# Depthwise convolution in 32x32 tiles of the PE array, with rows of h turned by DMA and PSUM in eight one-bank slots

## The chip, the cores and the metric

The kernel runs on one core of a Trainium2 chip. The metric is the device time of one execution in microseconds. Three runs of the kernel before gave 276.89, 278.99 and 280.02 us; their median is 278.99 us.

The engines are named as in the profile: PE (TensorE matmuls), PEld (its weight loads), DVE (VectorE), ACT (ScalarE), POOL (GpSimd) and SP (SyncE, which issues nearly all DMAs).

## The reference

Sliding-window attention (window 32 to both sides) over 8 batches, 8 heads, 576 positions and head dimension 64, and then a feed-forward block with a depthwise convolution of three taps along the sequence:

```python
scores = scale * np.matmul(q, k.transpose(0, 1, 3, 2))
mask = np.abs(pos[:, None] - pos[None, :]) <= 32
attn = softmax(np.where(mask, scores, -1e9))
x = np.matmul(attn, v)                       # to (8, 576, 512)

h = np.maximum(x @ w_in, 0.0)                # (8, 576, 1024)
conv_out = sum(conv_w[k] * shifted(h, k - 1) for k in range(3))   # per channel
gate = 1.0 / (1.0 + np.exp(-conv_out))
out = (h * gate) @ w_out                     # (8, 576, 512)
```

Inputs and the output are float32; the kernel multiplies in bf16.

## The kernel before

**Attention.** The heads of a batch are worked in four pairs `g`. `load_qk` and `load_v` bring float32 into staging tiles, POOL casts them to bf16 (`cast`). `job_tr` transposes the q or k of two pairs by nine matmuls against the identity each into one three-bank PSUM slot, and ACT and DVE copy one half each. (For batch 0 it does so in three pieces of 4, 4 and 1 blocks.) `job_sc` makes the scores of a pair, 18 matmuls of 64 rows, two heads one above the other in the array; ACT takes the exponential (1088 columns and 64), DVE multiplies by the band mask. `job_av` multiplies with v, 20 matmuls of 64 output columns; DVE normalises into `xn`. From batch 1 on, v shifted by 64 rows (`vo`) is made by two DMAs inside SBUF (`shift_v`). `job_xt` transposes `xn` into `xT`.

**Feed-forward.** The sequence of two batches is cut into three chunks `c` of 384 rows; there are twelve chunks. A chunk has eight blocks `m` of 128 channels. `job_ph` makes a block of h: four matmuls against `w_in`, and ACT's relu, halved, into `hT`. `job_pc` convolves the block: three matmuls, one for each tap, against a 128x128 diagonal matrix `diag_w` (built on DVE by `make_diag`, 24 in all), accumulated in PSUM; ACT takes the tanh into `tn`, and DVE forms the gated block `gT` = (`tn` + 1) * `hT`. Chunk 1 is worked in two halves of 192 columns. `job_py` makes 128 output rows: eight matmuls of `gT` against `w_out`, a copy by ACT into `y_sb`, and an output DMA.

**PSUM.** `psum_a` is one slot of three banks (transposes and scores), `psum_f` five slots of one bank (all else).

**Order.** The function `at` gives each job a planned time and the jobs that must come before it, and `give_out` emits the jobs by planned time. `P` = 29 is the planned time of a batch, `PC` = 2P/3 that of a chunk, and `dm` = `PC`/9 = 2.15. In the plan of a chunk, `ph` of block m stands at m `dm`, and the three outputs of the chunk before at 2.7, 5.3 and 7.9 `dm`. DMAs and POOL's casts keep this order. So do the compute engines for jobs planned before `T0` + 14 = 37 (`InOrder`, which is why early instructions carry line 87); later ones are ordered by the scheduler. Every engine executes its own list strictly in order, and so does SP: a DMA that waits holds up those behind it.

Of the kernel before, what the change touches and what calls it, by code (L numbers as in the profile page):

```python
# [17 lines left out]
def kernel(  # L18
# [51 lines left out]
    diag_w = consts.tile([128, 3, MB, 128], BF16, name="diag_w")  # L70
# [73 lines left out]
    conv_w24 = consts.tile([3 * MB, 128], FP32, name="conv_w24")  # L144
    nc.scalar.dma_start(conv_w24, moe_conv_w.rearrange("k (m p) -> (k m) p", p=128))
    make_identity(nc, ident)
    ident24 = consts.tile([3 * MB, 3 * MB], FP32, name="ident24")
    nc.vector.tensor_copy(out=ident24, in_=ident[0:3 * MB, 0:3 * MB])
    nc.vector.memset(mask1, 1.0)
# [30 lines left out]
    def load_weight(src, dst, rows, cast_):  # L180

        n = src.shape[1] // 2
        for x in (0, n):
            st = {}

            def load(x=x, st=st):
                t_ = fpool.tile([128, rows * n], FP32, name="wst", tag="wst")
                st[0] = t_.rearrange("p (c f) -> p c f", c=rows)
                fixed(nc.sync.dma_start(
                    st[0], src.rearrange("(c p) f -> p c f", p=128)[:, :, x:x + n]  # L190
                ))
# [9 lines left out]
    def slot_a():  # L201
        return psum_a.tile([128, 1536], FP32, name="pa", tag="pa")

    def slot_f():
        return psum_f.tile([128, 512], FP32, name="pf", tag="pf")
# [4 lines left out]
    def job_tr(g2, y):  # L210

        b, i = g2 // NPH, g2 % NPH
        nat = qkb_pp[b % NLD][y][i]
        to = []
        for g in (2 * g2, 2 * g2 + 1):
            if y == 0:
                t_ = apool.tile([128, S], BF16, name="qT", tag="qT", bufs=4)
                to.append(t_)
            else:
                t_ = kT_pp[g % NKT]  # L220
                to.append(t_[:, PAD:PAD + S])
            state["qk"[y], g] = t_

        small = b == 0
        for js in ((range(0, 4), range(4, 8), range(8, RP)) if small else (range(RP),)):
            j0, n = js[0], len(js)
            ps = slot_f() if small else slot_a()
            for j in js:
                tensor.matmul(  # L229
                    ps[:, 128 * (j - j0):128 * (j - j0) + 128],  # L230
                    nat[:, j, :, :].rearrange("p e d -> p (e d)"),
                    ident, start=True, stop=True,
                )
            rows = ps[:, 0:128 * n].rearrange("p (j y x) -> p y x j", j=n, y=2)
            for x, copy in enumerate((scalar.copy, vector.tensor_copy)):
                copy(  # L236
                    out=to[x].rearrange("p (x j) -> p x j", j=RP)[:, :, j0:j0 + n], in_=rows[:, x]
                )
# [9 lines left out]
    def col(e, t):  # L248

        return 512 * e + 64 * t if t < 8 else 1024 + 64 * e  # L250

    def job_sc(g):
        qT, kT = state.pop(("q", g)), state.pop(("k", g))
        ps, last = slot_a(), slot_f()
        for i in range(NT):
            for e, t in ((0, (i + NT - 1) % NT), (1, i)):
                tensor.matmul(  # L257
                    last[:, 0:64] if e * t == NT - 1 else ps[:, col(e, t):col(e, t) + 64],
                    kT[64 * e:64 * e + 64, 64 * t:64 * t + 128],
                    qT[64 * e:64 * e + 64, 64 * t:64 * t + 64],  # L260
                    start=True, stop=True,
                )
        attn = apool.tile([128, 2 * S], BF16, name="attn", tag="attn", bufs=4)
        state["a", g] = attn
        x = 2 * S - 64
# [99 lines left out]
    def job_pc(c, m, halves=(0, 1)):  # L365
        kind = c % 3
        step = HW + (2 if kind == 1 else 0)
        if m == 0 and halves[0] == 0:
            gT[c] = fpool.tile([128, MB, CH], BF16, name="gT", tag="gT", bufs=3)

        def taps(kk):
            base = hT_pp[kind][:, m, kk:kk + HW]
            return bass.AP(
                base.tensor, base.offset + step * halves[0],
                [list(base.ap[0]), [step, len(halves)], [1, HW]],
            )

        n = HW * len(halves)
        ps = slot_f()
        for kk in range(3):  # L380
            tensor.matmul(  # L381
                ps[:, 0:n], diag_w[:, kk, m, :], taps(kk), start=(kk == 0), stop=(kk == 2)
            )
        tn = spool.tile([128, CH], FP32, name="tn", tag="tn")
        scalar.activation(tn[:, 0:n], ps[:, 0:n], AF.Tanh, bias=0.0, scale=1.0)  # L385
        vector.scalar_tensor_tensor(  # L386
            out=gT[c][:, m, HW * halves[0]:HW * halves[0] + n].rearrange(
                "p (i x) -> p i x", x=HW),
            in0=tn[:, 0:n].rearrange("p (i x) -> p i x", x=HW), scalar=1.0, in1=taps(1),
            op0=ALU.add, op1=ALU.mult,  # L390
        )

    out_rows = out.rearrange("b s f -> (b s) f")

# [23 lines left out]
    def at(key, t, job, *before):  # L418
        assert key not in plan
        plan[key] = (t, job, before)  # L420
# [29 lines left out]
    def hidden(c, t, dt, part):  # L450
        halves = (0, 1) if part is None else (part,)
        kind = c % 3
        b0 = c // 3 * 2
        need = []
        if kind < 2 and part != 1:
            need += [("xt", b0, i) for i in (range(4) if kind == 0 else range(NBLK))]
        if kind and part != 0:
            need += [("xt", b0 + 1, i) for i in (range(2) if kind == 1 else range(NBLK))]
        for m in range(MB):
            at(("ph", c, m, part), t + m * dt, lambda m=m: job_ph(c, m, halves),  # L460
               *need, ("w_in", 2 * m // MB),
               *[("pc", c - 3, m, x) for x in (None, 0, 1)])
            at(("pc", c, m, part), t + (m + 1.4) * dt, lambda m=m: job_pc(c, m, halves),
               ("ph", c, m, part), ("diag", m), *[("py", c - 3, i) for i in range(3)],
               *[("pc", c, m, x) for x in (0,) if part == 1])

    for m in range(MB):
        at(("diag", m), (8.8, 9.0, 11.7)[m] if m < 3 else T0 + 1.6 * m - 1.5, lambda m=m: make_diag(m), ("conv_w",))
    at(("conv_w",), 7.0, job_conv_w)
    for c in range(NCH):  # L470
        if c == 0:
            hidden(0, T0, 1.6, None)
        elif c == 1:
            hidden(1, T0 + 13.0, 1.0, 0)
            hidden(1, start[1], 1.4, 1)
        else:
            hidden(c, start[c], dm, None)
        for i in range(3):
            t = start[c + 1] + (2.7 + 2.6 * i) * dm if c else T1 + 2.0 + 3.0 * i
            at(("py", c, i), t, lambda c=c, i=i: job_py(c, i),  # L480
               *[("pc", c, m, x) for m in range(MB) for x in (None, 0, 1)], ("w_out", 0), ("w_out", 1))


    pair = {}
# [58 lines left out]
    for i, (ld, cs) in enumerate(load_weight(moe_w_out, w_out_sb, MB, cast)):  # L543
# [33 lines left out]
```

## Time and profile before

| what | value |
|---|---|
| times of three runs | 276.89, 278.99, 280.02 us |
| median | 278.99 us |
| profiled execution | span 274.9 us from the first to the last instruction |
| PE busy | 243.0 us, 88% |
| DVE busy | 179.0 us, 65% |
| ACT busy | 174.4 us, 63% |
| POOL busy | 81.2 us, 30% |
| SP's DMA queue | 45.68 MB, 59.4% of the 16 DMA engines |
| mean granted PE clock | 0.988 |

The profile gives the execution's span alone; what lies around the span is seen from the median, which is 4.1 us longer. Times inside the profile count from the start of the span. A busy share is a mean over the whole span; the prediction reads the stages apart from each other, because the first 66 us, the steady part and the end have different limits.

### The profile page before, as it was taken

The page shows a single profiled execution, that of the slowest core. Times are in us where ns is not written, and L with a number is a line of the kernel's source. Part 1 is how long each engine was busy: PE and PEld are TensorE (multiplying, and loading weights), DVE is VectorE, ACT ScalarE, POOL GpSimd, SP SyncE. Part 2 cuts the span into 40 slices and gives each one's busy share as a digit, 9 for nine tenths or more (in the row PEclk, how much of TensorE's full clock was granted, in tenths as well). Part 3 has the DMA queues.
Part 4 walks back from the last instruction along what each step waited for, and adds up shares of the span by engine and source line. Part 5 has one row for each costly group of instructions (what it writes and reads, how often), then busy time and mean ns, then how long its engine had stood idle before and what let it go on. Part 6 is the DMA issues. An engine that isn't in the chain of part 4 may idle for free.

```text
span 274.9 us, 6658 instructions
## 1 busy us (share of the span) xinstructions
PE 243.0 (88%) x2654; PEld 149.9 (55%) x2682; DVE 179.0 (65%) x392; ACT 174.4 (63%) x370; POOL 81.2 (30%) x96
## 2 busy tenths in 40 slices
PE   0746975886999999999999999999999999999994
PEld 0625444564665665656566555565566655555551
DVE  5697385996567688687667858696576656623230
ACT  1756472575678667767777677576776766556552
POOL 5659666664125143134113503333200000000000
PEclk9999996899999999999999999999999999999999
DMA  6999999996486925956659556974241211112123
GB/s 244 242 294 387 211 305 326 222 316 151 124 200 244 247 62 114 251 192 171 155 154 310 150 123 162 270 195 118 67 118 38 74 43 41 42 38 76 41 76 114
DMA packets 55714, 46.11 MB, mean 168 GB/s; under 512 B 38892, under 2 KB 40964, under 8 KB 55684
## 3 DMA queue, kind: packets, MB, share of 16 engines
q1 hardware_dynamic: 55648, 45.68, 59.4%
q8 instruction: 21, 0.34, 0.5%
q14 instruction: 9, 0.07, 0.1%
q10 hardware_dynamic: 36, 0.01, 0.0%
HBM read 32.52 MB, written 9.44 MB: 153 GB/s over the span
## 4 chain that ended last, share of the span: by engine, by line
PE 69%; DMA 11%; DVE 8%; SPq 4%; ACT 3%; issue 3%; POOL 1%
PE pf L399 22%; PE pf L343 19%; PE pf L381 14%; DMA kst<-in_k_dram 5%; PE pa L229 4%; PE pf L282 4%; DMA vst<-in_v_dram 4%; SPq L95 3%; DMA vo<-ve 3%; PE pa L257 3%; PE pf L313 2%; DVE xT L318 2%; DVE attn L268 2%; DVE gT L386 1%; DVE gT L87 1%
## 5 line engine op out<-in xcount | busy, mean ns | idle before, releaser
L386 DVE SCALAR_TENSOR_TENSOR gT<-tn,hT 128x384 bf16<-128x384 f32 (+1 forms) x96 | 56.8, 599 | 45.9 <-ACT tn L385 45.5
L343 PE MATMUL pf<-xT,w_in_sb 128*128 128x385 bf16 (+2 forms) x380 | 73.4, 315 | 2.3 <-DVE xn L301 1.4
L399 PE MATMUL pf<-w_out_sb,gT 128*128 128x512 bf16 x260 | 65.6, 379 | 1.4
L381 PE MATMUL pf<-hT,diag_w 128*128 128x384 bf16 (+1 forms) x288 | 58.7, 313 | 0.7 <-ACT hT L354 0.6
L404 ACT COPY y_sb<-pf 128x512 f32<-128x512 f32 x36 | 21.1, 586 | 42.5 <-PE pf L399 40.2
L385 ACT ACTIVATE tn<-pf 128x384 f32<-128x384 f32 (+1 forms) x96 | 45.1, 470 | 4.2 <-PE pf L381 3.4
L343 PEld LDWEIGHTS <-w_in_sb 128*128 128x128 bf16 x380 | 33.9, 98 | 21.9 <-DVE xn L301 2.0
L399 PEld LDWEIGHTS <-gT 128*128 128x128 bf16 x288 | 27.8, 98 | 29.6 <-DVE gT L386 0.2
L109 POOL TENSOR_SCALAR ve<-vst 128x512 bf16<-128x512 f32 x40 | 29.3, 736 | 49.3 <-DMA vst<-in_v_dram 40.2
L381 PEld LDWEIGHTS <-diag_w 128*128 128x128 bf16 x288 | 25.8, 97 | 15.7 <-issue 1.1
L363 ACT ACTIVATE hT<-pf 128x385 bf16<-128x385 f32 x56 | 27.8, 497 | 8.7 <-PE pf L343 7.9
L266 ACT ACTIVATE attn<-pa 128x1088 bf16<-128x1088 f32 x26 | 28.0, 1076 | 5.6 <-PE pf L257 4.8
L109 POOL TENSOR_SCALAR kb<-kst 128x1152 bf16<-128x1152 f32 x16 | 20.2, 1262 | 29.3 <-DMA kst<-in_k_dram 16.3
L109 POOL TENSOR_SCALAR qb<-qst 128x1152 bf16<-128x1152 f32 x16 | 18.9, 1179 | 29.9 <-DMA qst<-in_q_dram 29.1
L268 DVE TENSOR_TENSOR attn<-attn,mask 128x1152 bf16<-128x1152 bf16 x26 | 22.3, 857 | 7.2 <-ACT attn L267 6.6
L301 DVE TENSOR_TENSOR xn<-pf,rec 128x320 bf16<-128x320 f32 x52 | 23.4, 480 | 0.4
L318 DVE CAST xT<-pf 128x512 bf16<-128x512 f32 (+1 forms) x32 | 19.2, 633 | 3.6 <-PE pf L313 3.5
L358 ACT ACTIVATE hT<-pf 128x386 bf16<-128x386 f32 x24 | 11.8, 499 | 5.4 <-PE pf L343 5.2
L282 PEld LDWEIGHTS <-attn 128*64 128x64 bf16 x520 | 10.6, 111 | 8.3 <-issue 6.0
L282 PE MATMUL pf<-ve,attn 128*64 128x65 bf16 x312 | 13.8, 197 | 0.5 <-DVE attn L268 0.3
L292 DVE RECIPROCAL rec<-pf 128x5 f32<-128x5 f32 x52 | 8.6, 181 | 7.8 <-PE pf L282 7.8
L257 PE MATMUL pa<-qT,kT 64*128 64x64 bf16 x442 | 12.5, 191 | 0.9 <-DVE kT L236 0.9
(84 smaller groups left out, 271.0 us busy)
## 6 DMA issues: line engine op xcount, KB each, us to landing
qst<-in_q_dram SPq DMA_DIRECT2D x16, 576.0 KB, 7.0
kst<-in_k_dram SPq DMA_DIRECT2D x16, 576.0 KB, 7.2
out_dram<-y_sb SPq DMA_DIRECT2D x36, 256.0 KB, 2.2
vst<-in_v_dram SPq DMA_DIRECT2D x24, 256.0 KB, 4.1
vo<-ve SPq DMA_DIRECT2D x14, 260.0 KB, 6.3
vst<-in_v_dram SPq DMA_DIRECT2D x16, 192.0 KB, 4.9
wst<-in_moe_w_in_dram SPq DMA_DIRECT2D x2, 1024.0 KB, 8.0
wst<-in_moe_w_out_dram SPq DMA_DIRECT2D x2, 1024.0 KB, 8.2
```

What stands on the lines that cost most here:

```text
L109: fixed(nc.gpsimd.tensor_scalar(out=out_, in0=in_, scalar1=1.0, scalar2=0.0, op0=ALU.mult, op1=ALU.add))
L266: scalar.activation(attn[:, 0:x], ps[:, 0:x], AF.Exp, bias=0.0, scale=scale)
L268: vector.tensor_tensor(out=attn, in0=attn, in1=mask, op=ALU.mult)
L282: tensor.matmul(pss[e][64 * j:64 * j + 64, 65 * c:65 * c + 65], attn[:, col(e, t):col(e, t) + 64], (ve if t % 2 == 0 else vo)[:, t // 2, h ...
L301: vector.tensor_tensor(out=to, in0=po[:, :, 0:64], in1=rec[:, :, None].broadcast_to([128, NBLK, 64]), op=ALU.mult,)
L318: (vector.tensor_copy if b > 1 or c % 2 else scalar.copy)(out=xT[b // 2][:, :, b % 2, 128 * c:128 * c + cols], in_=ps[:, :, 0:cols])
L343: tensor.matmul(ps[:, 0:n], w_in_sb[:, kc, m * 128:(m + 1) * 128], x_[:, kc, x0:x1], start=(kc == 0), stop=(kc == KC - 1),)
L363: scalar.activation(hT[:, m, o0:o0 + n], ps[:, 0:n], AF.Relu, bias=0.0, scale=0.5)
L381: tensor.matmul(ps[:, 0:n], diag_w[:, kk, m, :], taps(kk), start=(kk == 0), stop=(kk == 2))
L385: scalar.activation(tn[:, 0:n], ps[:, 0:n], AF.Tanh, bias=0.0, scale=1.0)
L386: vector.scalar_tensor_tensor(out=gT[c][:, m, HW * halves[0]:HW * halves[0] + n].rearrange("p (i x) -> p i x", x=HW), in0=tn[:, 0:n].rearr ...
L399: tensor.matmul(ps, gT[c][:, m, 128 * i:128 * i + 128], w_out_sb[:, m, :], start=(m == 0), stop=(m == MB - 1),)
```

## The change

- The convolution works four channel blocks at once (a quad `qd`). Each 128x128 diagonal matrix holds only four 32x32 diagonals that matter, so each tap of a block becomes four matmuls of 32 rows by 32 columns. Row group r of block m goes to column group (r + m) mod 4: the sixteen matmuls of a tap use sixteen different 32x32 tiles of the array, and the four row groups that share a column group write to four different PSUM banks.
- The channels of block m so come out turned by 32 (m mod 4) partitions. For three of the four blocks, `hT` is therefore copied into `gT` by two DMAs each, turned in the same way (`turn`), and DVE gates in place. The rows of `w_out` are turned when they are loaded: seven DMAs for each half instead of one.
- The quad needs four PSUM slots at once. `psum_a` goes, and `psum_f` has eight slots of one bank. Scores take four slots and four exponentials (512, 512, 64, 64 columns), and every `job_tr` works in three pieces as batch 0's did.
- `diag_w` is 32 wide and built by a single DVE instruction. `tn` has six buffers instead of three.
- In the plan, `pc` of quad `qd` stands at (4 `qd` + 4.4) `dm`.

```diff
-    psum_a = ctx.enter_context(tc.tile_pool(name="psum_a", bufs=1, space=bass.MemoryType.PSUM))
-    psum_f = ctx.enter_context(tc.tile_pool(name="psum_f", bufs=5, space=bass.MemoryType.PSUM))
+    psum_f = ctx.enter_context(tc.tile_pool(name="psum_f", bufs=8, space=bass.MemoryType.PSUM))
...
-    def make_diag(m):
-        for kk in range(3):
-            vector.tensor_scalar(
-                out=diag_w[:, kk, m, :], in0=ident,
-                scalar1=conv_w_sb[:, kk, m:m + 1], scalar2=None, op0=ALU.mult,
-            )
+    def make_diag():
+        vector.tensor_tensor(
+            out=diag_w.rearrange("p k m x -> p (k m) x"),
+            in0=ident32[:, None, :].broadcast_to([128, 3 * MB, 32]),
+            in1=conv_w_sb.rearrange("p k m -> p (k m)")[:, :, None].broadcast_to([128, 3 * MB, 32]),
+            op=ALU.mult,
+        )
...
+                rows_ = src.rearrange("(c p) f -> p c f", p=128)[:, :, x:x + n]
+                for s in range(4):
+                    for lo, to, cnt in turn(s):
+                        fixed(nc.sync.dma_start(
+                            st[0][to:to + cnt, s:rows:4, :], rows_[lo:lo + cnt, s:rows:4, :]
+                        ))
...
+    def turn(s):
+        return [(0, 32 * s, 128 - 32 * s), (128 - 32 * s, 0, 32 * s)][:2 if s else 1]
...
-        for js in ((range(0, 4), range(4, 8), range(8, RP)) if small else (range(RP),)):
+        for js in (range(0, 4), range(4, 8), range(8, RP)):
...
-        scalar.activation(attn[:, 0:x], ps[:, 0:x], AF.Exp, bias=0.0, scale=scale)
-        scalar.activation(attn[:, x:], last[:, 0:64], AF.Exp, bias=0.0, scale=scale)
+        for i, (x, n) in enumerate(((0, 512), (512, 512), (1024, 64), (1088, 64))):
+            scalar.activation(
+                attn[:, x:x + n], ps[i][:, 0:n], AF.Exp, bias=0.0, scale=scale
+            )
...
-        ps = slot_f()
+        ms = range(4 * qd, 4 * qd + 4)
+        for m in ms:
+            for lo, to, cnt in turn(m % 4) if m % 4 else []:
+                fixed(nc.sync.dma_start(gate(m, to, to + cnt), taps(m, 1, lo, lo + cnt)))
+        pss = [slot_f() for _ in ms]
         for kk in range(3):
-            tensor.matmul(
-                ps[:, 0:n], diag_w[:, kk, m, :], taps(kk), start=(kk == 0), stop=(kk == 2)
-            )
-        tn = spool.tile([128, CH], FP32, name="tn", tag="tn")
-        scalar.activation(tn[:, 0:n], ps[:, 0:n], AF.Tanh, bias=0.0, scale=1.0)
...
+            for ps, m in zip(pss, ms):
+                for r in range(4):
+                    o = 32 * ((r + m) % 4)
+                    tensor.matmul(
+                        ps[o:o + 32, 0:n], diag_w[32 * r:32 * r + 32, kk, m, :],
+                        taps(m, kk, 32 * r, 32 * r + 32), start=(kk == 0), stop=(kk == 2),
+                    )
+        for ps, m in zip(pss, ms):
+            tn = spool.tile([128, CH], FP32, name="tn", tag="tn", bufs=6)
+            scalar.activation(tn[:, 0:n], ps[:, 0:n], AF.Tanh, bias=0.0, scale=1.0)
+            vector.scalar_tensor_tensor(
+                out=gate(m), in0=tn[:, 0:n].rearrange("p (i x) -> p i x", x=HW), scalar=1.0,
+                in1=gate(m) if m % 4 else taps(m, 1), op0=ALU.add, op1=ALU.mult,
             )
...
+        for qd in range(MB // 4):
+            at(("pc", c, qd, part), t + (4 * qd + 4.4) * dt, lambda qd=qd: job_pc(c, qd, halves),
+               *[("ph", c, 4 * qd + m, part) for m in range(4)], ("diag",),
+               *[("py", c - 3, i) for i in range(3)],
+               *[("pc", c, qd, x) for x in (0,) if part == 1])
```

More of the change, by code (lines that the diff above doesn't have):

```diff
@@ L69 @@
     conv_w_sb = consts.tile([128, 3, MB], FP32, name="conv_w_sb")
-    diag_w = consts.tile([128, 3, MB, 128], BF16, name="diag_w")
+    diag_w = consts.tile([128, 3, MB, 32], BF16, name="diag_w")
+    ident32 = consts.tile([128, 32], BF16, name="ident32")
     ident = consts.tile([128, 128], BF16, name="ident")
@@ L146 @@
     make_identity(nc, ident)
+    for r in range(4):
+        nc.vector.tensor_copy(
+            out=ident32[32 * r:32 * r + 32, :], in_=ident[32 * r:32 * r + 32, 32 * r:32 * r + 32]
+        )
     ident24 = consts.tile([3 * MB, 3 * MB], FP32, name="ident24")
@@ L188, in load @@
                 st[0] = t_.rearrange("p (c f) -> p c f", c=rows)
-                fixed(nc.sync.dma_start(
-                    st[0], src.rearrange("(c p) f -> p c f", p=128)[:, :, x:x + n]
-                ))
+                rows_ = src.rearrange("(c p) f -> p c f", p=128)[:, :, x:x + n]
+                if not turned:
+                    fixed(nc.sync.dma_start(st[0], rows_))
+                    return
+                for s in range(4):
[3 more added lines that the diff above has]
+                        ))
             def casts(x=x, st=st):
@@ L250, in col, with bank @@
         return 512 * e + 64 * t if t < 8 else 1024 + 64 * e
+    def bank(e, t):
+        return (e, 64 * t) if t < 8 else (2 + e, 0)
     def job_sc(g):
         qT, kT = state.pop(("q", g)), state.pop(("k", g))
-        ps, last = slot_a(), slot_f()
+        ps = [slot_f() for _ in range(4)]
         for i in range(NT):
             for e, t in ((0, (i + NT - 1) % NT), (1, i)):
+                at_, x = bank(e, t)
                 tensor.matmul(
-                    last[:, 0:64] if e * t == NT - 1 else ps[:, col(e, t):col(e, t) + 64],
+                    ps[at_][:, x:x + 64],
                     kT[64 * e:64 * e + 64, 64 * t:64 * t + 128],
@@ L378, in job_pc, with gate @@
         n = HW * len(halves)
-        ps = slot_f()
-        for kk in range(3):
-            tensor.matmul(
-                ps[:, 0:n], diag_w[:, kk, m, :], taps(kk), start=(kk == 0), stop=(kk == 2)
-            )
-        tn = spool.tile([128, CH], FP32, name="tn", tag="tn")
[L385 to L390, printed above, removed]
-        )
+        def gate(m, p0=0, p1=128):
+            return gT[c][p0:p1, m, HW * halves[0]:HW * halves[0] + n].rearrange(
+                "p (i x) -> p i x", x=HW)
+        ms = range(4 * qd, 4 * qd + 4)
[3 more added lines that the diff above has]
+        pss = [slot_f() for _ in ms]
+        for kk in range(3):
+            for ps, m in zip(pss, ms):
+                for r in range(4):
+                    o = 32 * ((r + m) % 4)
+                    tensor.matmul(
+                        ps[o:o + 32, 0:n], diag_w[32 * r:32 * r + 32, kk, m, :],
+                        taps(m, kk, 32 * r, 32 * r + 32), start=(kk == 0), stop=(kk == 2),
+                    )
+        for ps, m in zip(pss, ms):
[4 more added lines that the diff above has]
+                in1=gate(m) if m % 4 else taps(m, 1), op0=ALU.add, op1=ALU.mult,
+            )
     out_rows = out.rearrange("b s f -> (b s) f")
@@ L461, in hidden @@
                *need, ("w_in", 2 * m // MB),
[L462 to L468, printed above, removed]
+               *[("pc", c - 3, m // 4, x) for x in (None, 0, 1)])
+        for qd in range(MB // 4):
[3 more added lines that the diff above has]
+               *[("pc", c, qd, x) for x in (0,) if part == 1])
+    at(("diag",), 8.8, make_diag, ("conv_w",))
     at(("conv_w",), 7.0, job_conv_w)
@@ L480 @@
             at(("py", c, i), t, lambda c=c, i=i: job_py(c, i),
-               *[("pc", c, m, x) for m in range(MB) for x in (None, 0, 1)], ("w_out", 0), ("w_out", 1))
+               *[("pc", c, qd, x) for qd in range(MB // 4) for x in (None, 0, 1)], ("w_out", 0), ("w_out", 1))
     pair = {}
```

18 lines of the change are left out of this document (7 added, 11 removed).

## The prediction

> **What bounds the kernel now.** I read the page's totals first, then the stretches, then the chain that ended last.
>
> ```profile
> span 274.9 us, 6658 instructions
> 45.00:66.00 21.00, 15.98 (x244) 11.79 (x240) 19.70 (x37) 13.01 (x32) 12.28 (x13) 0.89 1.05 280
> 83.50:142.00 58.50, 57.58 (x684) 34.78 (x692) 43.43 (x87) 40.65 (x81) 17.87 (x18) 1.00 0.62 169
> 142.00:200.50 58.50, 57.45 (x650) 34.44 (x657) 41.84 (x83) 40.40 (x82) 17.65 (x18) 1.00 0.67 182
> 200.50:240.00 39.50, 38.85 (x408) 23.28 (x413) 26.36 (x57) 26.32 (x54) 0.00 (x0) 1.00 0.16 52
> ```
>
> Columns of a stretch: its length, then busy time of PE, PEld, DVE, ACT and POOL, the granted clock, the DMA share and GB/s. From 66 us on PE has no gap worth naming. One period (two batches, three chunks of 384 rows) lasts 58.5 us; DVE works 42.6 us of it in the mean and ACT 40.5. Before 66 us it is another kernel: the DMA engines are full (share 1.05) and then DVE is (19.70 of 21). The chain of waits tells the same:
>
> ```profile
> 36.20 7.96 DMA vo<-ve
> 44.19 0.71 PE pf L87 x19
> 256.92 0.49 PE pf L381 x3
> 265.93 3.24 PE pf L399 x15
> 269.22 1.90 PE pf L399 x8
> 271.15 0.59 ACT y_sb L404
> ```
>
> A full convolution block (three 128x384 matmuls) takes 0.49 us of PE, 163 ns each, with its weight loads hidden. The run's median stands 278.99 - 274.9 = 4.1 us above this span; I sum against the span and add 4.1.
>
> **1. The convolution on PE.** Four blocks, 12 matmuls and 4 x 0.49 = 1.96 us, become 48 matmuls on 32x32 tiles, each with a weight load. No row shows a 32x32 tile. The nearest are two tiles side by side (the attention product, 64 output columns each) and two on top of each other (the scores, 64 rows each):
>
> ```profile
> 153.25 0.65 PE L381 MATMUL pf<-hT,diag_w 128*128 128x384 bf16 x3
> 153.83 0.39 PEld L282 LDWEIGHTS <-attn 128*64 128x64 bf16 x20 [0.32 <-issue]
> 153.83 0.22 PE L282 MATMUL pf<-ve,attn 128*64 128x65 bf16 x1
> 154.14 0.20 PE L282 MATMUL pf<-ve,attn 128*64 128x65 bf16 x2
> 154.27 0.32 PEld L257 LDWEIGHTS <-kT 64*128 64x128 bf16 x18
> 154.52 0.19 PE L257 MATMUL pf<-qT,kT 64*128 64x64 bf16 x1
> 154.63 0.12 PEld L343 LDWEIGHTS <-w_in_sb 128*128 128x128 bf16 x2
> ```
>
> Twenty pairs of load and matmul start within about 0.31 us, 15.5 ns a pair, while one 65-column stream at 163/384 ns a column needs 28 ns: two tiles do run together, and loads go beside them. 48 x 15.5 = 0.74 us. At best the sixteen tiles stream together, 3 x 0.163 = 0.49 us; at worst not at all beyond today's 1.96 or more (rival C). I take 0.74, the row it is nearest to. Each change of tile shape leaves a gap: the three matmuls end streaming at 153.25 + 0.49 = 153.74, the next load starts at 153.83. Two such gaps, 0.1 each: 0.94 us a quad (0.6 to 1.2), a gain of 1.0 us.
>
> The Trainium skill speaks against this order of issue. TensorE: Matmul & The Clock Gate, The mechanism (Part 3), says that a weight load overlaps running matmuls only when its row group differs; here the fifth pair is back on the first one's rows. In the attention product all tiles share all four row groups and the pairs still come every 15.5 ns, so the trace goes against it for side-by-side tiles; what the rule would make of the time is rival C.
>
> **2. Middle, 66 to 200.5 us (134.5 us, 2.3 periods).** Six quads a period: PE falls by 6 x 1.02 = 6.1 to 52.4 us. What is added elsewhere:
>
> ```profile
> L236 ACT CAST kT<-pa x12: 639/639/640, 63.7 to 218.4; 128x576 bf16<-128x576 f32 x12
> L236 DVE CAST kT<-pa x12: 745/758/758, 64.4 to 219.0; 128x576 bf16<-128x576 f32 x12
> 8.60 1.19 ACT L87 CAST kT<-pf 128x256 bf16<-128x256 f32 x3 [0.45 <-PE pf L87]
> 9.08 1.22 DVE L87 CAST kT<-pf 128x256 bf16<-128x256 f32 x3 [0.41 <-ACT kT L87]
> 10.54 1.08 ACT L87 ACTIVATE attn<-pa 128x1088 bf16<-128x1088 f32 x1 [0.75 <-PE pf L87]
> 11.51 0.22 ACT L87 ACTIVATE attn<-pf 128x64 bf16<-128x64 f32 x1
> ```
>
> Batch 0 already copies q and k in three pieces: 1.19 against 0.64 on ACT, 1.22 (1.09 in its other group) against 0.76 on DVE. Eight such copies a period: ACT +4.4, DVE +3.2. The exponentials go from 1088 + 64 columns to 512 + 512 + 64 + 64. From these two rows a column costs 0.84 ns and a following piece starts 0.1 us early, so two more pieces cost 0.12: eight pairs, ACT +1.0. That is 45.8 us for DVE and 45.9 for ACT, under PE's 52.4 but near 88% of it. The removed cover is the old conv blocks strewn between attention steps; PE will wait more often there.
>
> Then the new wait. The gating of three blocks of each quad waits for rows turned by DMA:
>
> ```profile
> 154.06 0.36 SPq L406 DMA_DIRECT2D out_dram<-y_sb  x1
> out_dram<-y_sb SPq DMA_DIRECT2D x36, 256.0 KB, 2.2
> vo<-ve SPq DMA_DIRECT2D x14, 260.0 KB, 6.3
> SPq L406 <- ACT y_sb L404: 132.1, 28, 6.7
> L386 DVE SCALAR_TENSOR_TENSOR gT<-tn,hT 128x384 bf16<-128x384 f32 x80 | 49.6, 625 | 40.7 <-ACT tn L385 40.3
> ```
>
> Six DMAs a quad (288 KB) at 0.36 us of SP each take 2.2 us to issue and land 2.2 us later on an empty queue, 6.3 behind loads as `vo` does. SP takes them in order, and mostly stands at an output DMA until `y_sb` is copied (132 us in all). For the first quad of a chunk the last output stands 1.7 `dm` (3.6 us) earlier in the plan, so the rows come nearly in time; for the second it is 0.5 `dm`, 1 us, and the last row piece comes some 5 us after the quad while tanh of its block is done after 3. On DVE, queued behind the waiting gating are masks, q/k copies and normalisation of the next pairs, for which PE waits. The instruction listing puts one to four such instructions between the gatings, which covers part. I take 1 us of stall a quad (0 to 2.5): 6 us a period, DVE 51.8. Three engines at 46 to 52.4 in order with each other: I take 55 us a period (52.4 to 60), a gain of 3.5 x 2.3 = 8 us (+14 to -3).
>
> Loads behind the turned rows on SP are late by some 3 us a group; costed at nothing, since `vo` is issued at 140.94 and the first product that reads it starts at 153.83:
>
> ```profile
> 140.94 1.11 SPq L136 DMA_DIRECT2D vo<-ve  x2
> ```
>
> It lands 6.3 us later, so 6 us of slack are left; gone, each batch would add the excess.
>
> **3. Front, up to 66 us.** The listing has the first quad's turned rows on SP behind batch 1's `vo` and four q/k loads of batch 2, each DMA waiting for the one eight before. The fifth and sixth pieces thus wait for loads, and all pass behind them.
>
> ```profile
> 39.11 0.76 SPq L103 DMA_DIRECT2D kst<-in_k_dram  x1
> 50.80 1.15 POOL L109 TENSOR_SCALAR kb<-kst 128x1152 bf16<-128x1152 f32 x1 [0.67 <-DMA kst<-in_k_dram]
> 39.88 1.16 DVE L87 TENSOR_TENSOR attn<-attn,mask 128x1152 bf16<-128x1152 bf16 x1
> 52.18 0.22 PE L87 MATMUL pf<-ve,attn 128*64 128x65 bf16 x1
> 60.89 0.22 PE L282 MATMUL pf<-ve,attn 128*64 128x65 bf16 x1
> 47.73 1.38 DVE diag_w L87 x3
> ```
>
> The last k load is there at 50.8, so the rows land near 52. In DVE's order the mask of batch 1's first pair (39.88 now) now stands behind that gating: about 53.7, and the product that starts at 44.19 starts at 53.7 too, +9.5. From there DVE sets the pace. It no longer builds diagonals (24 instructions become one; 1.4 us of this stretch), but has the longer copies. Adding up its listing with the durations above, the next pairs' products come at 57.0 (52.18 now) and 66.8 (60.89 now). I take +7 at the 66 us mark; +2 if the rows overtake the loads, +12 if the second quad's rows are late too. `w_out` in 14 DMAs costs SP 14 x 0.36 = 5 against 2 us; nothing, as the q/k loads land later anyway.
>
> **4. End.** Behind 200.5 us DVE has 26.36 of 39.5, so PE's gain stands: eight quads x 1.02 = 8 us (5 to 10). But the last quad's rows have nothing to hide behind: after the last but one output block SP waits for its copy (0.59), issues an output and six pieces (2.5), landing 2.2, gating 0.56, and 16 matmuls of the last two outputs follow. Counted from the end of that block, the last product comes at 9.6 instead of 5.7 us: +4 (2 to 6).
>
> **Sum.** 274.9 + 7 - 8 - 8 + 4 = 269.9; with 4.1 about 274 us, 5 below the median. The case's own range is 268 to 276.
>
> **Rivals.** One needs the duration of a narrow weight load:
>
> ```profile
> L282 PEld LDWEIGHTS <-attn x520: 106/111/114, 56.5 to 231.9; 128*64 128x64 bf16 x174
> ```
>
> A. PE stays the bound everywhere: rows land in time in the middle (gain 14), tail +2, front +3. For it: DVE has 45.8 of 52.4. Against: the listing's order. 274.9 + 3 - 14 - 8 + 2 + 4.1 = 262.
> B. Slower: DVE's wait for turned rows takes PE's place. It decides from (58.5 - 45.8)/6 = 2.1 us of stall a quad. For it: `vo` lands after 6.3 us, and the rows raise a DMA share of 0.62 to 0.67. Against: the listing's other work between gatings. At 3.2 us the period is 45.8 + 19.2 = 65: +15 over 2.3 periods, front +9: 274.9 + 9 + 15 - 8 + 4 + 4.1 = 299; a mild form (period 60) gives 287.
> C. The tiles don't do what is meant: four at a time, loads waiting for the rows above. 12 x (0.163 + about 0.1 for a load, whose row says 0.11 for 64 columns) = 3.2 us a quad, +1.2 on the 20 full quads behind the front, and no gain: 274.9 + 24 + 7 + 4 + 4.1 = 314. This is the skill's rule above; the 15.5 ns speak against it.
> D. Gain and loss cancel: the middle's periods shrink by under 1 us each, 2 in all: 274.9 + 7 - 2 - 8 + 4 + 4.1 = 280. For it: three engines near 46 to 52 us that wait for each other. Against: today's PE, which hardly waits at all with DVE at 42.6.
>
> **How the numbers follow.** Forecast 0.30, A 0.16, D 0.15, B 0.32, C 0.07. One per cent, 2.8 us, is about what a measurement of this kernel tells from no change. Faster is forecast and A, 0.46; the same is D, 0.15; slower is B and C, 0.39. The range takes in A and most of B, 261 to 295, and leaves out C, B's upper end and a little below A.
>
> **What would show it.** Right: a quad's 48 matmuls within 0.75 us, gaps of 0.1 around them; the first product of batch 1 near 54 us; periods of 55 us with DVE's idle time before L417 now ended by DMA for about 6 us of each; about 4 us of PE idle before the last outputs. Wrong: quads of 2 us or more (C), DVE waiting over 2 us a quad for DMA (B), or a front no later than now.

## The result, and the profile after

The changed kernel takes 304.95 us (median of 4 runs, 301.94 to 306.82), against 278.42 us before (4 runs, 276.89 to 280.02). The ratio is 1.093, with a 95% interval of 1.084 to 1.101: 26.5 us slower. An execution can fall into a slower state, as that of 306.82 us did: times in this document are medians of all executions, ratios and intervals leave the slower ones out. Forecast were 274.0 us and a range of 261 to 295; the outcome lies beside rival B's 299.

First the page of the kernel after: its totals, its engines, and the chain that ended last, by engine and by line.

```profile
span 300.2 us, 9124 instructions
PE 224.0 (75%) x3618; PEld 132.2 (44%) x3618; DVE 177.1 (59%) x429; ACT 180.7 (60%) x490; POOL 78.4 (26%) x96
DMA 32%; PE 28%; SPq 14%; DVE 10%; ACT 8%; issue 4%; POOL 2%; DVEq 0%; ACTq 0%
DMA gT<-hT 17%; PE pf L428 13%; SPq L404 10%; DMA kst<-in_k_dram 9%; PE pf L360 9%; DVE gT L417 4%; ACT y_sb L433 2%; DMA qst<-in_q_dram 2%; DMA vo<-ve 2%; PE pf L410 2%; DMA wst<-in_moe_w_out_dram 2%; DVE qT L248 2%; ACT attn L282 2%; SPq L200 2%; PE pf L299 1%
```

PE has 19 us less work (243.0 before), and still the span grew by 25.3 us. Each execution of after is 1.7 to 1.8 us longer than its own span, so less than half of the 4.1 us that the prediction added lies around the span; the rest is that the profiled execution of before was a quick one. No engine is busy more than 75%. The chain now runs through the turned rows: landing (`gT<-hT`, 17%) and issuing them on SP (L404, 10%) make up 27% of it.

To see where the time went, I mark the same work in both kernels: the copy of the first output of the first chunk, and that of the eighth. These are the timeline's rows on ACT, of before and then of after (start, duration, what it does, idle time before it and what ended that):

```profile
69.38 0.59 ACT L404 COPY y_sb<-pf 128x512 f32<-128x512 f32 x1 [1.40 <-PE pf L399]
...
205.65 0.59 ACT L404 COPY y_sb<-pf 128x512 f32<-128x512 f32 x1 [1.24 <-PE pf L399]
```

```profile
75.77 0.59 ACT L433 COPY y_sb<-pf 128x512 f32<-128x512 f32 x1 [1.14 <-PE pf L428]
...
228.22 0.59 ACT L433 COPY y_sb<-pf 128x512 f32<-128x512 f32 x1 [2.62 <-PE pf L428]
```

The marks cut the span into front, middle (seven chunks, with the attention of the batches beside them) and end. The stretches cut at them, middle and end of before, then middle and end of after (length, busy time of PE, PEld, DVE, ACT, POOL, granted clock, DMA share, GB/s):

```profile
69.38:205.65 136.27, 133.82 (x1558) 81.67 (x1574) 98.23 (x198) 94.55 (x195) 38.01 (x40) 1.00 0.64 173
205.65:274.90 69.25, 64.65 (x519) 36.28 (x526) 30.54 (x62) 41.88 (x84) 0.00 (x0) 1.00 0.16 58
```

```profile
75.77:228.22 152.45, 126.10 (x2098) 73.55 (x2096) 102.44 (x239) 100.97 (x276) 37.99 (x42) 0.98 0.66 184
228.22:300.20 71.98, 59.19 (x822) 30.31 (x820) 33.49 (x70) 41.57 (x98) 0.00 (x0) 1.00 0.28 89
```

The front is 6.4 us longer, the middle 16.2, the end 2.7: together the 25.3. In the middle PE works 7.7 us less, and its idle time goes from 2.5 to 26.4 us. What it waits for is one step away: DVE. These are the largest of PE's waits in the middle of after (us in total, times, longest); with the smaller ones, the waits that DVE ended make 25.9 of the 26.4 us:

```profile
PE pf L241 <- DVE xn L318: 6.4, 2, 4.9
PE pf L299 <- DVE qT L248: 4.5, 2, 2.7
PE pf L428 <- DVE gT L417: 3.5, 6, 1.0
PE pf L299 <- DVE attn L285: 2.1, 3, 0.9
```

Only the third is for the gating itself; the others are for normalised products (`xn`), copies of q and masks. The waits for the turned rows and the longest in the front, in the whole span, then the gating's in the middle alone and in the end alone:

```profile
DVE gT L417 <- DMA gT<-hT: 49.2, 37, 5.1
DVE gT L87 <- DMA gT<-hT: 16.3, 1, 16.3
PE pf L87 <- DVE attn L87: 18.6, 1, 18.6
```

```profile
DVE gT L417 <- DMA gT<-hT: 29.5, 19, 5.1
```

```profile
DVE gT L417 <- DMA gT<-hT: 19.6, 18, 2.9
```

One such wait in the chain, with what stands behind it:

```profile
87.18 0.80 SPq L404
...
88.02 3.56 DMA gT<-hT
...
91.70 0.28 DVE gT L417
...
92.14 0.76 DVE attn L285
...
92.94 0.51 PE pf L299 x20
```

and the same gating in DVE's timeline, with the idle time before it:

```profile
91.70 0.52 DVE L417 SCALAR_TENSOR_TENSOR gT<-tn,gT 128x192 bf16<-128x192 f32 x1 [1.73 <-DMA gT<-hT]
```

SP issues the first piece of the quad (one of half width) at 87.18, it lands at 91.58, DVE gates, and only then forms the attention mask (L285) for which PE's next attention product (L299) has waited. The mask has nothing to do with the convolution; it only stands behind the gating in DVE's list.

### The profile page after: what moved, and what is told of

It reads as the page before. It is cut to its first block, busy times and chain, and to the rows that moved or that the text cites. A ratio compares the mean times of both kernels' runs of the same rounds, so it can differ in the third digit from the quotient of the medians.

```text
span 300.2 us, 9124 instructions
## 1 busy us (share of the span) xinstructions
PE 224.0 (75%) x3618; PEld 132.2 (44%) x3618; DVE 177.1 (59%) x429; ACT 180.7 (60%) x490; POOL 78.4 (26%) x96
## 4 chain that ended last, share of the span: by engine, by line
DMA 32%; PE 28%; SPq 14%; DVE 10%; ACT 8%; issue 4%; POOL 2%; DVEq 0%; ACTq 0%
DMA gT<-hT 17%; PE pf L428 13%; SPq L404 10%; DMA kst<-in_k_dram 9%; PE pf L360 9%; DVE gT L417 4%; ACT y_sb L433 2%; DMA qst<-in_q_dram 2%; DMA vo<-ve 2%; PE pf L410 2%; DMA wst<-in_moe_w_out_dram 2%; DVE qT L248 2%; ACT attn L282 2%; SPq L200 2%; PE pf L299 1%
## 5 line engine op out<-in xcount | busy, mean ns | idle before, releaser
L428 PE MATMUL pf<-w_out_sb,gT 128*128 128x512 bf16 x288 | 72.3, 386 | 10.2 <-DVE gT L417 7.7
L417 DVE SCALAR_TENSOR_TENSOR gT<-tn,gT 128x384 bf16<-128x384 f32 (+1 forms) x72 | 41.8, 587 | 53.3 <-DMA gT<-hT 49.2
L109 POOL TENSOR_SCALAR ve<-vst 128x512 bf16<-128x512 f32 x40 | 28.6, 723 | 67.1 <-DMA vst<-in_v_dram 42.4
L416 ACT ACTIVATE tn<-pf 128x384 f32<-128x384 f32 (+1 forms) x96 | 37.5, 491 | 5.0 <-issue 2.5
L282 ACT ACTIVATE attn<-pf 128x512 bf16<-128x512 f32 (+1 forms) x104 | 35.8, 426 | 3.5 <-PE pf L273 3.1
L380 ACT ACTIVATE hT<-pf 128x385 bf16<-128x385 f32 x56 | 30.1, 556 | 13.0 <-PE pf L360 12.4
L109 POOL TENSOR_SCALAR qb<-qst 128x1152 bf16<-128x1152 f32 x16 | 18.6, 1162 | 37.6 <-DMA qst<-in_q_dram 36.7
L285 DVE TENSOR_TENSOR attn<-attn,mask 128x1152 bf16<-128x1152 bf16 x26 | 21.5, 825 | 7.4 <-ACT attn L282 7.2
L318 DVE TENSOR_TENSOR xn<-pf,rec 128x320 bf16<-128x320 f32 x52 | 24.9, 489 | 1.3
L410 PE MATMUL pf<-hT,diag_w 32*32 32x384 bf16 (+1 forms) x1152 | 21.5, 318 | 2.6 <-DVE qT L248 1.7
L299 PE MATMUL pf<-ve,attn 128*64 128x65 bf16 x312 | 13.6, 199 | 8.6 <-DVE qT L248 4.5
L87 ACT ACTIVATE attn<-pf 128x512 bf16<-128x512 f32 (+1 forms) x24 | 7.7, 438 | 19.7 <-PE pf L87 19.7
L299 PEld LDWEIGHTS <-attn 128*64 128x64 bf16 x520 | 10.8, 112 | 18.6 <-issue 10.0
L87 PE MATMUL pf<-ve,attn 128*64 128x65 bf16 x72 | 4.4, 237 | 18.6 <-DVE attn L87 18.6
L417 DVE SCALAR_TENSOR_TENSOR gT<-tn,hT 128x384 bf16<-128x384 f32 (+1 forms) x24 | 13.8, 573 | 7.2 <-ACT tn L416 7.2
L248 ACT CAST qT<-pf 128x256 bf16<-128x256 f32 (+1 forms) x36 | 13.4, 484 | 6.1 <-PE pf L241 6.1
```

The lines of the kernel that those rows point to most:

```text
L109: fixed(nc.gpsimd.tensor_scalar(out=out_, in0=in_, scalar1=1.0, scalar2=0.0, op0=ALU.mult, op1=ALU.add))
L282: scalar.activation(attn[:, x:x + n], ps[i][:, 0:n], AF.Exp, bias=0.0, scale=scale)
L299: tensor.matmul(pss[e][64 * j:64 * j + 64, 65 * c:65 * c + 65], attn[:, col(e, t):col(e, t) + 64], (ve if t % 2 == 0 else vo)[:, t // 2, h ...
L318: vector.tensor_tensor(out=to, in0=po[:, :, 0:64], in1=rec[:, :, None].broadcast_to([128, NBLK, 64]), op=ALU.mult,)
L410: tensor.matmul(ps[o:o + 32, 0:n], diag_w[32 * r:32 * r + 32, kk, m, :], taps(m, kk, 32 * r, 32 * r + 32), start=(kk == 0), stop=(kk == 2),)
L417: vector.scalar_tensor_tensor(out=gate(m), in0=tn[:, 0:n].rearrange("p (i x) -> p i x", x=HW), scalar=1.0, in1=gate(m) if m % 4 else taps( ...
```

## The experiments

The times of before on the chips of these runs are 278.5 us (E1 to E4), 279.8 (E5 to E8) and 279.0 (E9, E10, whose ratios go by 276.6). All kernels are cut at the same two marks:

| kernel | time, us | ratio, 95% interval | front | middle | end |
|---|---|---|---|---|---|
| before | 278.4 | 1 | 69.4 | 136.3 | 69.3 |
| after | 304.95 | 1.084 to 1.101 | 75.8 | 152.5 | 72.0 |
| E1 no turned rows | 268.2 | 0.959 to 0.968 | 69.1 | 132.9 | 63.7 |
| E2 turned rows unread | 268.3 | 0.959 to 0.969 | 67.8 | 134.4 | 63.7 |
| E3 PSUM part alone | 276.35 | 0.985 to 0.994 | 70.6 | 134.9 | 69.1 |
| E4 rows issued early | 274.9 | 0.982 to 0.991 | 69.4 | 139.0 | 63.5 |
| E5 outputs issued by ACT | 293.7 | 1.045 to 1.058 | 77.9 | 146.7 | 66.9 |
| E6 both | 287.5 | 1.021 to 1.035 | 71.1 | 148.2 | 65.3 |
| E7 early in the front only | 296.9 | 1.056 to 1.070 | 70.4 | 152.9 | 72.1 |
| E8 turned on PE | 272.3 | 0.967 to 0.980 | 69.1 | 135.9 | 67.1 |
| E9 E1 in pairs of blocks | 270.7 | 0.969 to 0.988 | 72.6 | 132.4 | 66.4 |
| E10 E8 in pairs of blocks | 272.2 | 0.977 to 0.993 | 67.0 | 133.6 | 68.5 |

### E1 and E2: without the wait

E1 issues no turned rows, and all blocks are gated with h as it stands:

```diff
-        for m in ms:
-            for lo, to, cnt in turn(m % 4) if m % 4 else []:
-                fixed(nc.sync.dma_start(gate(m, to, to + cnt), taps(m, 1, lo, lo + cnt)))
...
-                in1=gate(m) if m % 4 else taps(m, 1), op0=ALU.add, op1=ALU.mult,
+                in1=taps(m, 1), op0=ALU.add, op1=ALU.mult,
```

> The changed kernel without the 156 DMAs that turn rows of h: DVE gates all four blocks with h as it stands, so three of four blocks are gated with the wrong channels. All else is kept (tiles, PSUM slots, three-piece copies, four exponentials, w_out turned). Theory 1 (DVE waits for the turned rows, in order, and all else waits for DVE): PE is the bound again from 66 us on, front as before; span 274.9 - 14 - 8 = 253 to 262, time 257 to 266. Theory 2 (the PSUM cut and the extra copies and exponentials cost it): time 285 to 305.

E2 issues all 156 at the same place in the same order, into a tile that nobody reads:

```diff
-                fixed(nc.sync.dma_start(gate(m, to, to + cnt), taps(m, 1, lo, lo + cnt)))
+                fixed(nc.sync.dma_start(gate(m, to, to + cnt, gS), taps(m, 1, lo, lo + cnt)))
...
-                in1=gate(m) if m % 4 else taps(m, 1), op0=ALU.add, op1=ALU.mult,
+                in1=taps(m, 1), op0=ALU.add, op1=ALU.mult,
```

> As the kernel without turned rows, but the 156 DMAs are issued at their old places and write a tile that nothing reads; the gating again takes h as it stands. This keeps what the DMAs cost on SP and on the DMA engines and takes away DVE's wait alone. Theory 1 (DVE's wait itself): within 6 us of the kernel without the DMAs, 257 to 270. Theory 3 (SP blocked by 0.59 us an issue, loads and vo late, fuller DMA engines): 285 to 305, with PE's idle time ended by vo or by casts.

E1 took 268.2 us, 2 us above the range of its first theory and far below that of the second; E2 took 268.3, as its first theory had it. The two are the same: 156 more DMAs on SP's queue, their issue time and their traffic cost nothing that these times show. The whole difference to 304.95, 36.7 us, is that DVE reads what they bring. Middle of E2, as cut above:

```profile
67.79:202.15 134.36, 123.08 (x2080) 74.57 (x2096) 103.55 (x237) 100.99 (x276) 41.16 (x45) 0.97 0.78 218
```

The DMA share is higher here than in after (0.78 to 0.66) and PE waits less than half as long (11.3 us of 134.4).

### E3: the PSUM part alone

The kernel keeps the 128x128 convolution, block by block, and the plan of before; it has the eight one-bank slots, the three-piece copies and the four exponentials of the change.

```diff
-    psum_a = ctx.enter_context(tc.tile_pool(name="psum_a", bufs=1, space=bass.MemoryType.PSUM))
-    psum_f = ctx.enter_context(tc.tile_pool(name="psum_f", bufs=5, space=bass.MemoryType.PSUM))
+    psum_f = ctx.enter_context(tc.tile_pool(name="psum_f", bufs=8, space=bass.MemoryType.PSUM))
```

(against the kernel before; scores and transposes as in the change)

> The kernel before with its convolution in 128x128, and of the change only the eight one-bank slots, the three-piece q/k copies and the four exponentials. Theory 1: PE hides them, 277 to 285. Theory 2: a large part of the 26 us, 288 to 305.

It took 276.35 us, ratio 0.985 to 0.994. ACT has 184.7 us of work against 174.4, and the time is 0.6 to 1.5% lower, less than 2%, too little to build on: the longer copies and exponentials do lie under PE, as the prediction had it. The tiles with their order in quads, E3 to E1 without the rows they need, are worth 276.35 - 268.2 = 8 us.

### E4 and E7: the same rows, issued earlier

E4 issues the two DMAs of a block right behind its relu, in `job_ph`, instead of all six ahead of the quad (in the plan, a block of h then also waits for the outputs of three chunks before, whose `gT` it takes):

```diff
+        for lo, to, cnt in turn(m % 4) if m % 4 else []:
+            base = hT[lo:lo + cnt, m, 1:1 + HW]
+            fixed(nc.sync.dma_start(
+                gT[c][to:to + cnt, m, HW * halves[0]:HW * halves[0] + w].rearrange("p (i x) -> p i x", x=HW),
...
-        for m in ms:
-            for lo, to, cnt in turn(m % 4) if m % 4 else []:
-                fixed(nc.sync.dma_start(gate(m, to, to + cnt), taps(m, 1, lo, lo + cnt)))
```

> The changed kernel with the turned rows of a block issued on SP in the order of its relu (up to 3.4 dm earlier in the list) instead of at the head of its quad. Theory 1: most of the DVE wait behind the front goes (49 us of idle before L417 down to under 20), the front's 16 us wait stays; 280 to 293. Theory 3: SP still issues as much; 298 to 308.

It took 274.9 us, 0.9 to 1.8% below before, again too little to build on, but 30 us less than after. That is below the 280 to 293 expected: the front's wait, expected to stay at 16 us, halved too. Its waits of DVE for the rows, over the whole span:

```profile
DVE gT L421 <- DMA gT<-hT: 8.4, 4, 3.0
DVE gT L87 <- DMA gT<-hT: 8.3, 1, 8.3
```

Those are 16.7 us where after had 65.5. The end is that of E1; the middle is 2.7 us longer than before instead of 16.2.

E7 does this for the first two chunks only.

```diff
+        for lo, to, cnt in turn(m % 4) if m % 4 and c < 2 else []:
...
+            for lo, to, cnt in turn(m % 4) if m % 4 and c > 1 else []:
```

> The changed kernel with the early issue for chunks 0 and 1 only. It shows the front's share alone: first output near 69.5 us instead of 75.8 and the rest as in the changed kernel, so 297 to 301 if the two parts add up; near 305 if the later waits eat the front's gain; below 292 if the front's delay was what made the later rows late.

It took 296.9 us (297 to 301 expected if the two parts add up): by the medians 8 of the 30 us between after and E4 are the front's, by the profiled spans 5 of 28. Its front is repaired (70.4) and its middle and end are as long as those of after (152.9 and 72.1), so the two losses add up and neither hides the other. But DVE's waits for rows in its middle are 15.6 us, and 29.5 in after: a middle of the same length comes with half of them. Their sum alone does not give the time, and what else holds E7's middle is not shown.

### E5 and E6: what SP stands at

Ahead of the rows on SP stand the outputs, which wait for their copy. E5 lets ACT issue them, E6 does so on top of E4:

```diff
-        fixed(nc.sync.dma_start(out_rows[r0:r0 + 128, :], y_sb))
+        fixed(nc.scalar.dma_start(out_rows[r0:r0 + 128, :], y_sb))
```

> The changed kernel with its 36 output DMAs issued by ACT, behind its own copy of y_sb, so that SP no longer stands at an output before it issues turned rows. Theory 1a (the rows are late because SP waits at outputs in front of them): most of the 49 us of DVE idle behind the front goes, 280 to 290. Theory 1b (they are late because the DMAs are issued only at the head of the quad, 3.5 us of issue and 3 us of landing): DVE's wait stays above 35 us, 297 to 306. Each output costs ACT about 0.6 us of issue, 20 us of 300 in all.

> The kernel with early turned rows (274.93 us) and its output DMAs on ACT. If SP's standing at outputs is what is left of the wait there: 266 to 271, near the kernel without turned rows. If not, or if ACT's issue costs as much: 273 to 280.

E5 took 293.7 us, outside the ranges of both its theories. Its waits for rows behind the front nearly go away; the front's wait stays:

```profile
DVE gT L417 <- DMA gT<-hT: 7.3, 6, 3.3
DVE gT L87 <- DMA gT<-hT: 16.7, 1, 16.7
```

So behind the front it was SP's standing at the outputs that made the rows late. But the middle still lasts 146.7 us, and E6 takes 287.5, 12.6 us more than E4 (about 11.6 by the ratios). Moving the outputs thus costs something of its own in the middle, 9 us from E4 to E6 (139.0 to 148.2). The expectation for E6 was missed. An output holds ACT for 0.34 us in E6, not for the 0.6 expected, 12 us for all 36. Another part may show in its chain:

```profile
181.10 0.59 ACT y_sb L437
181.72 6.19 DMA out_dram<-y_sb
187.93 4.26 DMA gT<-hT
192.27 0.69 DVE gT L421
```

By this chain a turned row starts only when an output has landed, 6.2 us after ACT issued it (the median of its outputs is 2.3). In the waits of E6 this occurs five times with 15.9 us of SP's time. The middles of E4 and then of E6 show where the 9 us are:

```profile
69.44:208.46 139.02, 122.81 (x2079) 73.62 (x2096) 102.14 (x239) 100.62 (x276) 41.49 (x45) 0.98 0.78 217
71.13:219.33 148.20, 127.99 (x2098) 75.08 (x2096) 102.30 (x239) 101.63 (x276) 41.11 (x45) 0.95 0.74 203
```

PE is idle for 4.0 us more and busy for 5.2 us more, at a lower granted clock. In E4 the clock is 0.50 and then 0.66 from 183 to 190 us, around the end of a wait of PE of 4.55 us, and 1.00 from 190; E6 has two such stretches, 84 to 92 (0.51, 0.64) with a wait of 2.54 us and 190 to 198 (0.50, 0.66) with one of 4.51. How much the issue on ACT and the wait for landings each make isn't settled.

### E8: turned by PE

No rows are turned by DMA. Twelve more 32x32 matmuls a quad, against the identity, put h turned into three more PSUM slots, from which DVE gates:

```diff
+                for r in range(4):
+                    o = 32 * ((r + m) % 4)
+                    tensor.matmul(
+                        turned[m][o:o + 32, 0:n], ident32[32 * r:32 * r + 32, :],
+                        taps(m, 1, 32 * r, 32 * r + 32), start=True, stop=True,
+                    )
...
-                in1=gate(m) if m % 4 else taps(m, 1), op0=ALU.add, op1=ALU.mult,
+                in1=(turned[m][:, 0:n].rearrange("p (i x) -> p i x", x=HW)
+                     if m % 4 else taps(m, 1)), op0=ALU.add, op1=ALU.mult,
```

> The changed kernel without the DMAs: h is turned by twelve more 32x32 matmuls a quad against the identity, into three further PSUM slots, and DVE gates from PSUM. PE pays 12 x 15.5 ns = 0.19 us a quad, 5 us in all. If the wait for the DMAs was the whole cause: 268.2 + 5 = 270 to 276. If seven of eight PSUM slots in one quad make PE wait for ACT and DVE: 280 to 295.

It took 272.3 us (270.74 to 273.82), ratio 0.967 to 0.980, and beats both kernels. What a quad now costs PE, from its chain:

```profile
166.71 0.74 PE pf L407 x48
167.45 0.36 PE pf L417 x12
```

The turn costs 0.36 us of PE a quad, twice the 0.19 expected, and no wait of DVE is put down to it. That a quad takes seven of the eight PSUM slots does not bring the 280 to 295 us of the second theory.

### E9 and E10: why the middle gains so little even without the wait

E1's middle is only 3.4 us shorter than before. PE's work fell by 11.9 us, its idle time rose from 2.5 to 11.0:

```profile
69.07:201.97 132.90, 121.92 (x2080) 74.20 (x2097) 100.41 (x237) 100.51 (x275) 36.05 (x41) 0.97 0.63 178
```

The longest of its waits, in the timelines of PE and of DVE:

```profile
178.58 1.47 PE L360 MATMUL pf<-xT,w_in_sb 128*128 128x386 bf16 x4 [4.53 <-DVE xT L335]
```

```profile
175.02 2.90 DVE L414 SCALAR_TENSOR_TENSOR gT<-tn,hT 128x384 bf16<-128x384 f32 x4
...
177.84 1.87 DVE L335 CAST xT<-pf 128x512 bf16<-128x512 f32 x3
```

PE waits for `xT`, whose copy stands behind four gatings in a row (2.90 us). The granted clock is 0.76 from 178 to 185 us, behind this wait, and 1.00 from 185 to 205. E9 tests whether such bunching is the reason: E1 with two blocks at once instead of four, each pair planned as soon as its h is there. E10 is the same for E8.

```diff
-        ms = range(4 * qd, 4 * qd + 4)
+        ms = range(2 * qd, 2 * qd + 2)
...
-            at(("pc", c, qd, part), t + (4 * qd + 4.4) * dt, lambda qd=qd: job_pc(c, qd, halves),
+            at(("pc", c, qd, part), t + (2 * qd + 2.4) * dt, lambda qd=qd: job_pc(c, qd, halves),
```

> The kernel without turned rows (three of four blocks gated with the wrong channels), with two blocks convolved at once instead of four, each pair of blocks as soon as its h is there. What is tested is why even without the wait the middle gains little: from the first output of the first chunk to that of the eighth it takes 132.9 us, 136.3 in the kernel before, while the prediction's PE sum would have taken 14 us off. Theory 1: the bunching costs it. Four tanhs (4 x 0.52) and four gatings (4 x 0.6) stand in one block on ACT and DVE, and attention behind them waits. Then pairs, with half the block, shrink the middle to 126 to 131 us and the time to 261 to 266. Theory 2: bunching doesn't matter, DVE and ACT with their added pieces do; then the pairs, which cost PE up to 0.4 us more for four blocks (eight tiles are back after 8 x 15.5 = 124 ns, a stream lasts 163, and one gap more), give 268 to 274.

> The kernel that turns h on PE, with two blocks convolved at once instead of four; correct result. Theory 1 (bunching costs): below 270, to 264. Theory 2 (only PE's added cost counts): 273 to 278.

E9 took 270.7 us with a middle of 132.4, E10 272.2 with 133.6. Middle of E9, and then a pair in its chain:

```profile
72.60:205.01 132.41, 126.21 (x2101) 72.54 (x2120) 103.84 (x239) 102.42 (x277) 36.49 (x40) 0.99 0.64 179
```

```profile
166.92 0.61 PE pf L407 x24
```

Both theories were half right. Unbunched, PE's idle time falls from 11.0 to 6.2 us; but a pair takes 0.61 us, 1.22 for four blocks against 0.74, and PE's work rises by 4.3. One eats the other. By its time E9 falls to theory 2; E10's lies between the two and decides nothing. By the ratios neither gains on its quad version: E9's interval lies wholly above E1's, and E10's overlaps with E8's. What makes the other 6.2 us of idle time in E9 was not tested.

## Why the prediction was wrong, step by step

**The tiles (step 1): right.** A quad takes the 0.74 us forecast; in E4's and E8's chains stand 0.74 us for 48 matmuls, 15.4 ns a pair of load and matmul. (That is the quickest and commonest value at full width; some entries there are longer, up to 1.12 us, at a granted clock of 1.00 too.) Without the wait PE's work in middle and end fell by 11.9 + 7.7 = 19.6 us (E1: 121.92 of 133.82, and 56.91 of 64.65), where the sum had 14 + 8. Rival C, four tiles at a time, is out. In TensorE: Matmul & The Clock Gate, The mechanism (Part 3), the Trainium skill lets a weight load overlap only where the row group differs; here every fifth pair is back on the same row group and the 15.4 ns stay, so the trace goes against it as a limit on the rate. With one stream of 163 ns to a row group at a time, the 48 would need 48 x 163 / 4 ns = 1.96 us.

**The added pieces (step 2): hidden as forecast, and smaller.** E1's middle has 100.4 us of DVE and 100.5 of ACT; forecast were 45.8 and 45.9 for 58.5 us of progress, which makes 107 for the whole middle. Against before, DVE's work rose by 2.2 us where the sum had about 7.5, ACT's by 6.0 where it had about 12.6. E3 shows them hidden.

**The front (step 3): right.**

```profile
51.36 2.49 DVE L87 SCALAR_TENSOR_TENSOR gT<-tn,gT 128x384 bf16<-128x384 f32 x3 [16.29 <-DMA gT<-hT]
53.77 0.75 DVE L87 TENSOR_TENSOR attn<-attn,mask 128x1152 bf16<-128x1152 bf16 x1
```

Forecast were rows at 52, the mask behind them at 53.7, and +7 us at the 66 us mark; at the first mark it is +6.4, and E7 removes 5.4 of it. How long a wait would be was worked out here by walking through SP's list, and it held.

**The middle's stall (step 2): the step that failed.** "I take 1 us of stall a quad (0 to 2.5)" and "I take 55 us a period": both the size of the stall and the way it was turned into time were wrong. The middle has twelve full quads and two of half width, and 29.5 us of waiting: 2.1 us each, double the value taken and inside its bounds, on the very point from which rival B was to decide. 152.45/136.27 x 58.5 gives a period of 65.4 us; B had 65. Instead of -8 us the middle brought +16. Two of its terms were too small. The rows' issue and landing on SP, from the tile's own view (ns, minimum, median, maximum; then us to landing):

```profile
L404 SPq DMA_DIRECT2D gT<-hT x156: 472/594/2044, 42.6 to 292.1; - x156
DMA to landing us min/median/max: 1.7/3.0/9.5
```

A piece takes 0.594 us to issue; 0.36 was taken from the outputs, though the prediction itself quoted two DMAs inside SBUF at 1.11 us. Six pieces are 3.6 us, and with 3.0 to land, 6.6 instead of 4.4. And the cover was overrated: "work between gatings" doesn't help when the gating stands ahead of it in the list. The mask shown above was held up by 1.7 us in that way.

The price of a microsecond of stall was underrated too. The prediction added the stall to DVE's busy time: with 2.1 us a quad that sum is 45.8 + 6 x 2.1 = 58.4 us a period, no more than the 58.5 of before, and the period became 65.4. DVE has 102 us of work in the middle, so a sum of busy times leaves room for 29.5 us of waiting in the 132.9 us of E1; the middle still grew by 152.5 - 132.9 = 19.6. In these traces a wait in DVE's list is not paid from its mean slack: PE is out of work when the waiting instruction stands ahead of a mask, a copy or a normalisation that it needs, as its waits above show. A fixed price for a microsecond of such waiting doesn't follow, as E7's middle shows.

**The end (step 4): the second miss.** "Behind 200.5 us DVE has 26.36 of 39.5, so PE's gain stands" - it doesn't, for the same reason. The rows come late there too: by the profile DVE waits 19.6 us for them, next to nothing in the first two of the eight quads and 2.1 to 4.2 us in each of the other six. The last quad shows it: SP, and what DVE and PE make of it, from the chain.

```profile
287.98 0.59 ACT y_sb L433
...
288.59 0.34 SPq L435
...
288.98 0.53 SPq L404
...
291.47 0.59 SPq L404
...
292.11 2.04 DMA gT<-hT
...
294.28 0.57 DVE gT L417
...
294.90 1.48 PE pf L428 x6
```

Copy, output, the pieces, landing, gating, last products: the path is the one worked out for the tail. From the end of the block before it (287.95) to that of the last product (296.38) it takes 8.4 us, 9.6 forecast, 5.7 before. The +4 was +2.7. But the prediction let only the last quad wait, and six of the eight do. PE's work in the end did fall, by 5.5 us, and its idle time rose from 4.6 to 12.8. The ends of E1, without the wait, and of E4, with the rows issued early, are 5.5 and 5.7 us shorter than that of before.

**The rivals.** B had the mechanism and the place. That its 299 lies near 304.95 is in part luck: for its period of 65 it put in 3.2 us of stall a quad, where the trace has 2.1 at a higher price; its front (+9) is 2.6 us too long, and its end (-8 + 4) 6.7 us too short. A (262) was refuted by E1: with no wait at all the time is 268, with PE idle for 11 us of the middle. Bunching is a part of that, since pairs of blocks (E9) leave 6.2 us. D needed a middle 2 us shorter, and it is 16 us longer. The 274 forecast is by coincidence what E4 measures, where the rows are in time for most quads.

## What to carry to other kernels

When a step on an in-order engine gets a new producer, walk through the lists for every instance, from the issue on the producer's queue to whatever stands behind the waiting instruction; don't size the stall by a round number or by the engine's idle share. Here the walk was carried through for the front and the last quad, where it held to 2 us; for the middle it stopped at a rounded 1 us a quad, and the middle came out 24 us longer than forecast. Issue a transfer as soon as its source exists, or move the data on an engine that has room for it and need not wait for a DMA: turning h by twelve small matmuls (0.36 us a quad) beats turning it by six DMAs that take 6.6 us to arrive.

## What the runs showed of the hardware that was not expected

- A DMA that turns rows inside SBUF holds SP for 0.594 us in the median; an output of 256 KB holds SP for 0.36 us, and ACT for 0.34 (E6).
- Added traffic alone costs nothing measurable here: with 156 DMAs more, E2 has 0.78 of the DMA engines' time in the middle where E1 has 0.63, and takes 268.3 us against 268.2.
- Eight 32x32 tiles in turn (E9) are slower per block than sixteen: 0.61 us for 24 matmuls, 25 ns each, against 15.4 ns; one 128x128 block takes 0.49 us, so a pair of blocks gains 0.37 us and a quad 1.22.
- Each of four waits of PE of 4.5 to 5.0 us goes with a lower granted clock around or behind its end: 0.60 from 173 to 177 us in after, 0.76 from 178 to 185 in E1, 0.50 to 0.66 in E4 and E6. Of the shorter waits some do (2.54 us in E6) and some don't (2.90 us, ending at 249.8 in E6, with 1.00 beside it). Part of what a long wait costs may thus be counted as PE's busy time.
